# Low-part subtractions on GpSimd or VectorE, and the accumulators as halves of one tile, in a thresholded-attention and gated-mix kernel

## The chip, the cores and the metric

The kernel runs on one core of a Trainium2 chip. A core has five engines with queues of their own, each of which works through its instructions in order: TensorE (PE in the profile; PEld are its weight loads), VectorE (DVE), ScalarE (ACT), GpSimd (POOL) and SyncE (SP), which here only issues DMAs. Matrix products are summed in PSUM, everything else lies in SBUF. Engines wait for each other through semaphores: a counter that the one raises and the other waits for.

The metric is the device time of one execution in microseconds, as a median of several runs. The profile is of one execution.

## What is computed

```python
def _attn_ref(q, k, v, tau):                     # 8 batches, 8 heads, 576 x 64
    scale = 1.0 / np.sqrt(q.shape[-1])
    scores = scale * np.matmul(q, k.transpose(0, 1, 3, 2))
    thresh = np.max(scores, axis=-1, keepdims=True) - tau
    scores = np.where(scores >= thresh, scores, -1000000000.0)
    scores = scores - np.max(scores, axis=-1, keepdims=True)
    attn = np.exp(scores)
    attn = attn / (np.sum(attn, axis=-1, keepdims=True) + 1e-09)
    return np.matmul(attn, v)

def _moe_ref(x, w_val, conv_w, w_out):           # x: the heads side by side, 8 x 576 x 512
    ...
    for k in range(K):                           # K = 5, a causal convolution by channel
        gate_pre += conv_w[k][None, None, :] * xp[:, k:k + S, :]
    gate = 1.0 / (1.0 + np.exp(-gate_pre))
    val = x @ w_val
    return gate * val @ w_out
```

## The kernel before

Heads are worked in pairs: 8 batches of 4 pairs are 32 jobs. A job has 9 tiles of 128 query rows (four for each head, one for the 64 rows left over of both). For each tile PE multiplies queries by keys into a score tile `s` (L498), DVE takes the row maximum (L502), ACT the exponentials (L508) and the threshold (L510), DVE keeps the values over the threshold and sums them into `pp` or `pl` (L524), POOL or ACT divides (L554, L550), PE transposes by 128 columns into `tp` (L604) and ACT copies the result to `T` (L615). When half of a job's rows are there (320 or 256), PE multiplies `T` by `v` into an accumulator `acc` (L643, L650), and ACT evacuates it to `xT` (L658), the transposed output of the attention.

Then comes the mix, by batch. Each `xT` goes through the convolution's five taps (POOL L693, DVE L700) and the gate (ACT L708). PE makes two rounds of eight products of 12 matmuls each (L742): x by `w_val`, of which DVE makes g, gate times value (L769), and g by `w_out`, which ACT evacuates to `o` (L807). These too sum into `acc`, 320 or 256 columns at a time. So `acc` is written by 64 attention halves and 128 products, and is evacuated 192 times: 64 times by ACT L658, 64 by DVE L769, 64 by ACT L807.

Products are in float32 accuracy from parts of lower precision: a number is split into a high part (a rounded copy, made by ACT) and a low part (the number less its high part). `subtract` (L280 to L293) makes the low part, in two halves by column, of the keys (`kl`), the queries (`ql`), the attention's output (`xl`) and g (`gl`): 4 x 32 subtractions, 256 halves, all on POOL (L287).

No order is written out by hand. `op` notes an operation with the engines that may run it, a cost on each, a due time, what it comes after, and which buffers ("rooms") it takes and gives back. `carry_out` then plays it through with these costs: of all that can begin, it takes what can begin first, and among those the one with the earliest due time; the instructions are issued in that order. Where an operation has several ways (`other`), it goes to the engine on which it can begin first. POOL and the operations marked DVEp share one `port`: in the plan, only one of them runs at a time.

`Rooms` are buffers of one kind. `r_acc` has two tiles of 128 x 512 in PSUM, `acc0` and `acc1`; `take` hands out the one that came free first, `give` takes it back. The semaphore waits are not written in the kernel: the layer below adds them when it records the instructions, by which tile each reads and writes.

Of the kernel before, what the change touches and what calls it, by code (L numbers as in the profile page):

```python
# [10 lines left out]
F32 = mybir.dt.float32  # L11
# [4 lines left out]
ALU = mybir.AluOpType  # L16
# [5 lines left out]
DIVIDE = ("ACT",)  # L22
DUE = (8, 8, 8)
PACE_M = 0.17
# [3 lines left out]
def tile_thresholded_attention_gated_mix(  # L28
# [213 lines left out]
    class Words:  # L242


        def __init__(self, u, name, w, c, d0, before):
            due = u * 3.0 - 4
# [33 lines left out]
    def subtract(due, n, get, after, takes=(), gives=()):  # L280


        w = n // 2
        for cols in (slice(0, w), slice(w, n)):
            def run(cols=cols):
                dst, whole, high = get()
                nc.gpsimd.tensor_sub(dst[:, cols], whole[:, cols], high[:, cols].bitcast(F32))  # L287

            cost = w * 0.00237 + 0.04
            after = [op("POOL", due, cost, cost + 0.1, run, after, takes)]  # L290
            takes = ()
        after[0].gives = list(gives)
        return after[0]  # L293


    class Job:


        def __init__(self, i, b, g, at):
            self.i, self.b, self.g, self.at = i, b, g, at  # L300
            due = at - 9

            def fetch_v():
                self.v = r_v.take()
                nc.sync.dma_start(self.v, vs[b, g])

            self.got_v = op("SP", at - 3, 0.5, 3.6, fetch_v, takes=[r_v])
            if i == 0:
                self.load_at_once()
            else:  # L310
                self.prepare(due)

        def prepare(self, due):
# [28 lines left out]

            def scale_q():
                nc.gpsimd.tensor_scalar(self.q_r, self.q_r, sc, 0.0, op0=ALU.mult, op1=ALU.add)
# [5 lines left out]
            scaled = op("POOL", due, 0.75, 0.86, scale_q, [got_q])  # L350
            high = op("ACT", due + 1, 0.58, 0.76, high_q, [scaled], [r_qh])
            low = subtract(due + 2, S, low_q, [high], [r_ql], [(r_qr, lambda: self.q_r)])
# [94 lines left out]
    class Tile:  # L447
        def __init__(self, k, t, h, qc, grp):
# [21 lines left out]
            if TH == "ACT":  # L470
                after = [op("ACT", k - DUE[1], 0.83, 1.0, self.weigh, [largest], [r_e])]
            else:
                after = [
                    op("ACT", k - DUE[1], 0.64, 0.78, self.weigh, [largest], [r_e]),
                    op("DVE", k - 9, 0.13, 0.13, self.level, [largest]),
                ]
# [8 lines left out]
        def multiply(self):  # L485
            t, h, qc = self.t, self.h, self.qc
            s = self.s = r_s.take()
            for a in range(2):
# [17 lines left out]
        def weigh(self):  # L506
            self.e = r_e.take()
            nc.scalar.activation(self.e, self.s[:, :, :HS], AF.Exp, bias=self.nm[:, 0:1])  # L508
            if TH == "ACT":
                nc.scalar.activation(  # L510
                    self.nm[:, 1:2], self.nm[:, 0:1], AF.Identity, bias=less, scale=-1.0
                )

# [16 lines left out]
    class Group:  # L530
# [5 lines left out]
        def turned(self, k):  # L536
# [4 lines left out]
            add = op("POOL", k - 4, 0.2, 0.33, lambda: nc.gpsimd.tensor_scalar(  # L541
                sums(), sums(), 1.0, 1e-9, op0=ALU.mult, op1=ALU.add), [self.kept])
            inv = op("DVE", k - 4.9, 0.08, 0.33, lambda: nc.vector.reciprocal(ri(0, n), sums()), [add])  # L543
# [15 lines left out]
            for i in range(n):  # L559
                divided.append(op(  # L560
                    "POOL", k - 4 + 0.1 * i, 0.74, 0.82, divide(i, "POOL"), [inv],
# [3 lines left out]
            if self.both:  # L565
                divided.append(op("POOL", k - 4, 0.21, 0.3, lambda: spread(
# [3 lines left out]
            for c0, m in parts:  # L570
# [3 lines left out]
                    "PE", k - 3 + 0.1 * c0, 0.109 * m, 0.109 * (m - 1) + 0.35, self.turn(c0, m),  # L574
# [5 lines left out]
                if not half.begun:  # L580
                    takes, half.begun = [r_T], True
                out.append(op(
                    "ACT", k - 3 + 0.1 * c0, cost, cost + 0.17, self.copy(c0, m), [turn, *half.room], takes,
# [47 lines left out]
    class Half:  # L631
# [4 lines left out]
        def attended(self, k):  # L636
# [3 lines left out]
            def attend():  # L640
                acc = self.acc = r_acc.take()
# [17 lines left out]

            cost = 5 * w / 600 + 0.19  # L660
            gives = [(r_T, lambda: self.T)]
            if j == 1:
                gives.append((r_v, lambda: t.v))
            made = op("PE", k - 2, cost, cost + 0.2, attend, [t.got_v, *self.copies], [r_acc], gives)
            cost = 0.31 if j == 0 else 0.255
            after = [made] if j == 0 else [made, t.got_x]
            t.got_x = op("ACT", k - 4, cost, cost + 0.2, evacuate, after, [r_xT] if j == 0 else [],
                         [(r_acc, lambda: self.acc)])
# [185 lines left out]
    for t in jobs:  # L854
# [16 lines left out]
        convolve(t, batch, len(tiles))  # L871
        if t.g == NP - 1:
            last = products(batch, len(tiles) + 4.0, last)
# [44 lines left out]
```

## Time and profile before

| | |
|---|---|
| median of three runs | 766.35 us (765.61 to 766.81) |
| the profiled execution | 766.39 us |
| its span, first to last instruction | 764.6 us |
| busy: PE, DVE, ACT, POOL | 714.2, 617.5, 640.9, 544.1 us |
| mean granted clock of TensorE | 0.990 |

The page gives busy time, share of the span and the number of instructions for each engine; then the span in 40 slices of 19 us with the busy share of each in tenths; then groups of instructions by line, with busy time, mean length, and the idle time of the engine before them with what ended it. Records of PE's matmuls overlap, since the next begins before the last has left the array, so that "busy" tells that PE had work, not how fast it went.

### The profile page before, as it was taken

Reading aid. Unit: us, or ns where it says so; the run is one execution under the profiler, and the core shown is the slowest. Engines: PE = TensorE matmul, PEld = TensorE weight load, DVE = VectorE, ACT = ScalarE, POOL = GpSimd, SP = SyncE. Lnnn points to the kernel's source line nnn. Section 1 sums busy time; section 2 is a strip of 40 time slices with the busy share of each in tenths; the row PEclk is TensorE's granted clock in tenths of the full one; section 3 lists DMA queues with packets and bytes.
Section 4 is the critical chain, followed back from the end, with each engine's and each line's share of the span. In section 5 each row is a group of like instructions: output and inputs, shape, how many; then the busy total and the mean of one; then the engine's idle time right before and its main releaser. Section 6 shows DMA issues by size and latency. Waiting matters only on the chain.

```text
span 764.6 us, 15851 instructions
## 1 busy us (share of the span) xinstructions
PE 714.2 (93%) x5216; PEld 602.7 (79%) x5216; DVE 617.5 (81%) x1308; ACT 640.9 (84%) x1469; POOL 544.1 (71%) x885
## 2 busy tenths in 40 slices
PE   3687889979999999999999999999999999999997
PEld 3465557767788888888888888888888888888897
DVE  5878999989888878888888787888778988888630
ACT  5788987888889989989998898899889898988832
POOL 3677777778778867787678776688668876775431
PEclk9989999999999999999999999999999999999999
DMA  6746635344665556555555456455455455540001
GB/s 186 182 127 162 168 106 121 109 116 122 177 169 135 129 145 155 154 120 127 141 141 130 124 141 171 123 130 151 123 141 135 125 147 156 141 107 20 32 32 63
DMA packets 51890, 99.05 MB, mean 130 GB/s; under 512 B 9056, under 2 KB 9056, under 8 KB 51808
## 3 DMA queue, kind: packets, MB, share of 16 engines
q1 hardware_dynamic: 51488, 97.47, 49.0%
q8 instruction: 42, 0.69, 0.4%
q10 hardware_dynamic: 320, 0.56, 0.3%
q14 instruction: 40, 0.33, 0.1%
HBM read 35.74 MB, written 9.44 MB: 59 GB/s over the span
## 4 chain that ended last, share of the span: by engine, by line
PE 71%; DVE 8%; ACT 7%; POOL 6%; DMA 4%; issue 3%; SPq 1%; POOLq 0%; ACTq 0%
PE acc L742 20%; PE s L498 17%; PE acc L650 15%; PE tp L604 14%; PE acc L643 4%; DVE nm L502 3%; DMA q_r<-qT 2%; DVE pp L524 2%; ACT e L508 2%; ACT T L615 1%; DVE pre L700 1%; POOL pp L554 1%; POOL xl L287 1%; DMA KL<-kl 1%; POOL gl L287 1%
## 5 line engine op out<-in xcount | busy, mean ns | idle before, releaser
L502 DVE TENSOR_REDUCE nm<-s 128x1 f32<-128x576 f32 x288 | 215.8, 753 | 54.0 <-PE s L498 50.4
L508 ACT ACTIVATE e<-s,nm 128x576 f32<-128x576 f32 x288 | 215.5, 748 | 25.1 <-DVE nm L502 13.0
L524 DVE SCALAR_TENSOR_TENSOR pp<-s,nm,e 128x576 f32<-128x576 f32 x256 | 207.3, 813 | 35.1 <-ACT nm L510 31.7
L615 ACT COPY T<-tp 128x384 f32<-128x384 f32 x384 | 175.3, 487 | 27.6 <-PE tp L604 26.0
L604 PE MATMUL tp<-ident,pp 128*128 128x128 f32 x1152 | 182.3, 277 | 13.0 <-POOL pp L554 6.6
L498 PE MATMUL s<-KH,Q 128*128 128x288 f32 x512 | 162.1, 332 | 19.2 <-DVE Q L434 8.8
L554 POOL TENSOR_SCALAR pp<-pp,sums 128x576 f32<-128x576 f32 x174 | 142.5, 824 | 36.5 <-DVE sums L543 25.2
L604 PEld LDWEIGHTS tp<-ident,pp 128*128 128x128 f32 x1152 | 139.3, 142 | 23.2 <-POOL pp L554 10.1
L498 PE MATMUL s<-KL,Q 128*128 128x288 f32 x512 | 145.9, 299 | 0.7 <-DMA KL<-kl 0.7
L650 PE MATMUL acc<-T,v 128*64 128x256 f32 (+1 forms) x1024 | 138.3, 412 | 0.0
L498 PEld LDWEIGHTS s<-KH,Q 128*128 128x128 f32 x512 | 99.2, 194 | 43.3 <-DVE pp L524 13.8
L700 DVE SCALAR_TENSOR_TENSOR pre<-xT,cw,pre 128x576 f32<-128x576 f32 x128 | 119.2, 931 | 11.1 <-POOL pre L693 11.0
L650 PEld LDWEIGHTS acc<-T,v 128*64 128x64 f32 x1024 | 67.8, 136 | 62.9 <-issue 24.9
L498 PEld LDWEIGHTS s<-KL,Q 128*128 128x128 f32 x512 | 99.1, 194 | 0.9 <-DMA KL<-kl 0.9
L510 ACT ACTIVATE nm<-nm,less 128x1 f32<-128x1 f32 x288 | 85.0, 295 | 0.0
L742 PE MATMUL acc<-gl,woh 128*128 128x320 f32 (+1 forms) x256 | 78.1, 305 | 4.1 <-POOL gl L287 4.1
L742 PE MATMUL acc<-xl,wvh 128*128 128x320 f32 (+1 forms) x256 | 78.7, 307 | 2.6 <-POOL xl L287 2.5
L541 POOL TENSOR_SCALAR sums<-sums 128x2 f32<-128x2 f32 (+1 forms) x160 | 47.5, 297 | 45.5 <-DVE pp L524 33.2
L742 PE MATMUL acc<-gh,woh 128*128 128x320 f32 (+1 forms) x256 | 78.9, 308 | 0.7 <-ACT o L807 0.7
L742 PE MATMUL acc<-xh,wvl 128*128 128x320 f32 (+1 forms) x256 | 79.3, 310 | 0.0
L742 PE MATMUL acc<-xh,wvh 128*128 128x320 f32 (+1 forms) x256 | 78.4, 306 | 0.7 <-DVE g L769 0.5
L742 PE MATMUL acc<-gh,wol 128*128 128x320 f32 (+1 forms) x256 | 78.4, 306 | 0.0
(79 smaller groups left out, 1273.9 us busy)
## 6 DMA issues: line engine op xcount, KB each, us to landing
KH<-kh SPq DMA_DIRECT2D x124, 144.0 KB, 2.5
KL<-kl SPq DMA_DIRECT2D x124, 144.0 KB, 3.2
k_r<-kT SPq DMA_DIRECT2D x32, 320.0 KB, 3.7
v<-vs SPq DMA_DIRECT2D x32, 320.0 KB, 3.0
q_r<-qT SPq DMA_DIRECT2D x32, 288.0 KB, 2.9
outT<-o SPq DMA_DIRECT2D x32, 288.0 KB, 2.2
Q<-qh SPq DMA_DIRECT2D x62, 128.0 KB, 2.3
Q<-ql SPq DMA_DIRECT2D x62, 128.0 KB, 2.5
```

The lines of the kernel that those rows point to most:

```text
L498: nc.tensor.matmul(s[:, a, :HS], w, m, start=i == 0, stop=i == len(terms) - 1)
L502: nc.vector.tensor_reduce(self.nm[:, 0:1], self.s[:, :, :HS], axis=AX.XY, op=ALU.max, negate=True)
L508: nc.scalar.activation(self.e, self.s[:, :, :HS], AF.Exp, bias=self.nm[:, 0:1])
L510: nc.scalar.activation(self.nm[:, 1:2], self.nm[:, 0:1], AF.Identity, bias=less, scale=-1.0)
L524: nc.vector.scalar_tensor_tensor(grp.p[:, i * S : (i + 1) * S].rearrange("p (a f) -> p a f", a=2), self.s[:, :, :HS], self.nm[:, 1:2], self.e,
L541: add = op("POOL", k - 4, 0.2, 0.33, lambda: nc.gpsimd.tensor_scalar(sums(), sums(), 1.0, 1e-9, op0=ALU.mult, op1=ALU.add), [self.kept])
L554: nc.gpsimd.tensor_scalar(v, v, ri(i), 0.0, op0=ALU.mult, op1=ALU.add)
L604: nc.tensor.transpose(tp[:, i * P : (i + 1) * P], self.p[:, k0 : k0 + P], ident)
L615: nc.scalar.copy(T[:, c0 : c0 + n, self.off : self.off + P], tp[:, 0 : n * P].rearrange("p (c q) -> p c q", q=P),)
L650: nc.tensor.matmul(acc[hs, :w], t.v[:, c0 : c0 + D], T[:, h * NKC + c, :], start=False, stop=c == NKC - 1, skip_group_check=True,)
L700: nc.vector.scalar_tensor_tensor(cv, t.xT[:, i : i + S], cw[:, g, i : i + 1], cv, op0=ALU.mult, op1=ALU.add)
L742: nc.tensor.matmul(taken[name, e, j][:, :w], wt[:, c, c0 : c0 + P], moving(c, i)[:, hs], start=n == 0, stop=n == NM - 1,)
```

## The change

The two halves of each low-part subtraction get a second way, VectorE (as DVEp, with a cost of its own). The planner sends each half to the engine on which it can begin first. The diff carries more, of which most is switched so that it does what was done before: `EXTRA = 0`, `QS = False`, and constants (`AHEAD_D`, `LATE_M` and the like) with the values that stood in the code. One thing besides is not a switch: `r_acc` is now made of one tile of 128 x 2 x 512, and the two rooms that are handed out are its halves.

```diff
+SUB = True
+EXTRA = 0
+QS = False
...
-    r_s = Rooms(ps_s, 2, [P, 2, 512], F32, "s")
+    retired = []
+    r_s = Scores(ps_s, 2, [P, 2, 512], F32, "s")
     r_tp = Rooms(ps_t, 2, [P, 512], F32, "tp")
-    r_acc = Rooms(ps_a, 2, [P, 512], F32, "acc")
+    r_acc = Rooms(ps_a, 1, [P, 2, 512], F32, "acc")
+    if EXTRA:
+        r_s.extra = r_acc.take()
+        r_s.give(r_s.extra, 0.0)
+    else:
+        accs = r_acc.take()
+        for i in range(2):
+            r_acc.give(accs[:, i, :], 0.0)
...
         for cols in (slice(0, w), slice(w, n)):
-            def run(cols=cols):
+            def run(engine, cols=cols):
                 dst, whole, high = get()
-                nc.gpsimd.tensor_sub(dst[:, cols], whole[:, cols], high[:, cols].bitcast(F32))
+                engine.tensor_sub(dst[:, cols], whole[:, cols], high[:, cols].bitcast(F32))

             cost = w * 0.00237 + 0.04
-            after = [op("POOL", due, cost, cost + 0.1, run, after, takes)]
+            fast = w * 0.00116 + 0.07
+            after = [op(
+                "POOL", due, cost, cost + 0.1, lambda run=run: run(nc.gpsimd), after, takes,
+                other=[("DVEp", fast, fast + 0.12, lambda run=run: run(nc.vector))] if SUB else [],
+            )]
```

Lines move by the diff: L498 becomes L553, L604 L664, L658 L718, L742 L803, L769 L830, L807 L868, L287 L320. Of the 256 halves, 56 stand on VectorE in the new order (9 `kl`, 11 `ql`, 13 `xl`, 23 `gl`); four divisions move from POOL to ACT. With other costs in play the planner's whole order shifts: on every engine most rows stand elsewhere than before.

PE where the seventh batch's products by `w_val` reach their last block of columns (the first of its matmuls takes `xh0`; the row ahead of it is the last matmul of the product before). Names carry buffer numbers, and a bracket names the engine whose semaphore an instruction waits for. Before:

```order
L742 MATMUL acc1_106<-xh3_145,wvl_98 128x256
L742 MATMUL acc0_105<-xh0_142,wvh_97 128x320
L742 MATMUL acc0_105<-xl0_148,wvh_97 128x320
L604 MATMUL tp1_104<-ident_96,pl0_132 128x128 [waits Activation_49,Pool_49]
L742 MATMUL acc0_105<-xh0_142,wvl_98 128x320
L742 MATMUL acc0_105<-xh1_143,wvh_97 128x320
L742 MATMUL acc0_105<-xl1_149,wvh_97 128x320
L498 MATMUL s1_102<-KH0_117,Q0_115 128x288 [waits DVE_49]
```

The same place now:

```order
L803 MATMUL acc0_105<-xh3_144,wvl_98 128x256
L803 MATMUL acc0_105<-xh0_141,wvh_97 128x320
L803 MATMUL acc0_105<-xl0_147,wvh_97 128x320
L803 MATMUL acc0_105<-xh0_141,wvl_98 128x320
L803 MATMUL acc0_105<-xh1_142,wvh_97 128x320
L803 MATMUL acc0_105<-xl1_148,wvh_97 128x320 [waits DVE_49]
L553 MATMUL s1_102<-KH0_116,Q0_114 128x288
```

Both accumulators now have one name, `acc0_105`. The fifth matmul of the new product waits for DVE: by the semaphore's count, for the evacuation (L830) of the product before, which lies in the other half. That evacuation waits for PE to have done the fourth matmul of the new product, where before it waited for the twelfth of its own.

PE near the end of the program, where the products by `w_out` of the last batch follow each other without other work between them. Before, from one product's last three matmuls to the next one's first three:

```order
L742 MATMUL acc0_105<-gh3_161,woh_99 128x320
L742 MATMUL acc0_105<-gl3_165,woh_99 128x320
L742 MATMUL acc0_105<-gh3_161,wol_100 128x320
L742 MATMUL acc1_106<-gh0_158,woh_99 128x256 [waits Activation_49]
L742 MATMUL acc1_106<-gl0_162,woh_99 128x256
L742 MATMUL acc1_106<-gh0_158,wol_100 128x256
```

Now:

```order
L803 MATMUL acc0_105<-gh3_160,woh_99 128x320
L803 MATMUL acc0_105<-gl3_164,woh_99 128x320
L803 MATMUL acc0_105<-gh3_160,wol_100 128x320
L803 MATMUL acc0_105<-gh0_157,woh_99 128x256
L803 MATMUL acc0_105<-gl0_161,woh_99 128x256
L803 MATMUL acc0_105<-gh0_157,wol_100 128x256 [waits Activation_49]
```

The wait for ACT moved from the first matmul to the third, and it is for another evacuation: before, for the one of this same tile two products earlier; now for that of the product just finished.

The low parts of the last batch's g. Before, POOL's last rows of work:

```order
L693 TENSOR_SCALAR pre1_155<-xT1_141,cw0_172 128x576
L287 TENSOR_TENSOR xl1_149<-xT1_141,xh1_143 128x288 x2
L287 TENSOR_TENSOR gl0_162<-g0_156,gh0_158 128x288 x2
L287 TENSOR_TENSOR gl1_163<-g1_157,gh1_159 128x288 x2
L287 TENSOR_TENSOR gl2_164<-g0_156,gh2_160 128x288 x2
L287 TENSOR_TENSOR gl3_165<-g1_157,gh3_161 128x288 x2
```

Now DVE's last rows of work:

```order
L320 TENSOR_TENSOR gl0_161<-g0_155,gh0_157 128x288
L830 SCALAR_TENSOR_TENSOR g1_156<-pre1_154,acc0_105 128x320
L830 SCALAR_TENSOR_TENSOR g1_156<-pre1_154,acc0_105 128x256
L320 TENSOR_TENSOR gl1_162<-g1_156,gh1_158 128x288
L830 SCALAR_TENSOR_TENSOR g0_155<-pre1_154,acc0_105 128x320
L830 SCALAR_TENSOR_TENSOR g0_155<-pre1_154,acc0_105 128x256
L320 TENSOR_TENSOR gl2_163<-g0_155,gh2_159 128x288
L830 SCALAR_TENSOR_TENSOR g1_156<-pre1_154,acc0_105 128x320
L830 SCALAR_TENSOR_TENSOR g1_156<-pre1_154,acc0_105 128x256
L320 TENSOR_TENSOR gl3_164<-g1_156,gh3_160 128x288 x2
```

Five of these eight halves are DVE's now, one of each of the first three blocks and both of the last; POOL keeps three.

More of the change, by code (lines that the diff above doesn't have):

```diff
@@ L22 @@
 DIVIDE = ("ACT",)
+SUB = True
+EXTRA = 0
+QS = False
 DUE = (8, 8, 8)
+AHEAD_D = 4
+AHEAD_T = 3
+AHEAD_A = 2
+AHEAD_J = 9
+LATE_X = 0
+LATE_M = 4.0
+CONVERT = (3.0, -4)
 PACE_M = 0.17
@@ L176, in carry_out, with __init__, give @@
         assert not any(open_ops.values()), "some operations can never begin"
-    r_s = Rooms(ps_s, 2, [P, 2, 512], F32, "s")
-    r_tp = Rooms(ps_t, 2, [P, 512], F32, "tp")
-    r_acc = Rooms(ps_a, 2, [P, 512], F32, "acc")
+    class Scores(Rooms):
+        def __init__(self, *args):
+            super().__init__(*args)
+            self.extra = None
+        def give(self, room, when):
+            if self.extra is not None and room is self.extra and retired:
+                self.extra = None
+                for i in range(2):
+                    r_acc.give(room[:, i, :], when)
+            else:
+                super().give(room, when)
+    retired = []
+    r_s = Scores(ps_s, 2, [P, 2, 512], F32, "s")
+    r_tp = Rooms(ps_t, 2, [P, 512], F32, "tp")
+    r_acc = Rooms(ps_a, 1, [P, 2, 512], F32, "acc")
+    if EXTRA:
+        r_s.extra = r_acc.take()
+        r_s.give(r_s.extra, 0.0)
+    else:
+        accs = r_acc.take()
+        for i in range(2):
+            r_acc.give(accs[:, i, :], 0.0)
     r_kr = Rooms(raw, 1, [P, SK], F32, "k_r")
@@ L341, in low_q, with high_scaled, low_scaled @@
                 return self.ql, self.q_r, self.qh
+            def high_scaled():
+                self.qh = r_qh.take()
+                nc.scalar.mul(self.qh, self.q_r, sc)
+            def low_scaled():
+                self.ql = r_ql.take()
+                nc.vector.scalar_tensor_tensor(
+                    self.ql, self.q_r, sc, self.qh.bitcast(F32), op0=ALU.mult, op1=ALU.subtract
+                )
             def scale_q():
@@ L349, in prepare @@
             self.low_k = subtract(due + 1, SK, low_k, [self.high_k], [r_kl], [(r_kr, lambda: self.k_r)])
-            scaled = op("POOL", due, 0.75, 0.86, scale_q, [got_q])
-            high = op("ACT", due + 1, 0.58, 0.76, high_q, [scaled], [r_qh])
-            low = subtract(due + 2, S, low_q, [high], [r_ql], [(r_qr, lambda: self.q_r)])
+            if QS:
+                high = op("ACT", due + 1, 0.6, 0.78, high_scaled, [got_q], [r_qh])
+                low = op("DVEp", due + 2, 0.74, 0.87, low_scaled, [high], [r_ql], [(r_qr, lambda: self.q_r)])
+            else:
+                scaled = op("POOL", due, 0.75, 0.86, scale_q, [got_q])
+                high = op("ACT", due + 1, 0.58, 0.76, high_q, [scaled], [r_qh])
+                low = subtract(due + 2, S, low_q, [high], [r_ql], [(r_qr, lambda: self.q_r)])
             def place(which):
@@ L472, in __init__ @@
             else:
+                ways = {"ACT": (0.19, 0.33, self.level_act), "DVE": (0.13, 0.2, self.level)}
+                first, *rest = TH
                 after = [
                     op("ACT", k - DUE[1], 0.64, 0.78, self.weigh, [largest], [r_e]),
-                    op("DVE", k - 9, 0.13, 0.13, self.level, [largest]),
+                    op(first, k - 8.5, *ways[first], [largest], other=[(w, *ways[w]) for w in rest]),
                 ]
@@ L487, in multiply @@
             s = self.s = r_s.take()
+            if self.k >= EXTRA:
+                retired.append(self.k)
             for a in range(2):
@@ L540, in turned @@
             ri = lambda i, m=1: self.sums[:, 2 + i : 2 + i + m]
-            add = op("POOL", k - 4, 0.2, 0.33, lambda: nc.gpsimd.tensor_scalar(
+            add = op("POOL", k - AHEAD_D, 0.2, 0.33, lambda: nc.gpsimd.tensor_scalar(
                 sums(), sums(), 1.0, 1e-9, op0=ALU.mult, op1=ALU.add), [self.kept])
-            inv = op("DVE", k - 4.9, 0.08, 0.33, lambda: nc.vector.reciprocal(ri(0, n), sums()), [add])
+            inv = op("DVE", k - AHEAD_D - 0.9, 0.08, 0.33, lambda: nc.vector.reciprocal(ri(0, n), sums()), [add])
             divided = []
@@ L582, in turned @@
                 out.append(op(
-                    "ACT", k - 3 + 0.1 * c0, cost, cost + 0.17, self.copy(c0, m), [turn, *half.room], takes,
+                    "ACT", k - AHEAD_T + 0.1 * c0, cost, cost + 0.17, self.copy(c0, m), [turn, *half.room], takes,
                     [(r_tp, lambda c0=c0: self.tp[c0])],
@@ L640, in attend @@
             def attend():
-                acc = self.acc = r_acc.take()
+                acc = self.acc = rooms.take()
                 T = self.T[:, :, 0:w]
@@ L658, in evacuate @@
                 nc.scalar.copy(t.xT[:, x0 : x0 + w], self.acc[:, :w])
+            rooms = r_tp if EXTRA and t.b == 0 and k < EXTRA + 4 else r_acc
             cost = 5 * w / 600 + 0.19
@@ L663, in attended @@
                 gives.append((r_v, lambda: t.v))
-            made = op("PE", k - 2, cost, cost + 0.2, attend, [t.got_v, *self.copies], [r_acc], gives)
+            made = op("PE", k - AHEAD_A, cost, cost + 0.2, attend, [t.got_v, *self.copies], [rooms], gives)
             cost = 0.31 if j == 0 else 0.255
             after = [made] if j == 0 else [made, t.got_x]
-            t.got_x = op("ACT", k - 4, cost, cost + 0.2, evacuate, after, [r_xT] if j == 0 else [],
-                         [(r_acc, lambda: self.acc)])
+            t.got_x = op("ACT", k - AHEAD_A - 2, cost, cost + 0.2, evacuate, after, [r_xT] if j == 0 else [],
+                         [(rooms, lambda: self.acc)])
     class Batch:
@@ L870, in tile_thresholded_attention_gated_mix @@
             half.attended(len(tiles) - 1)
-        convolve(t, batch, len(tiles))
+        convolve(t, batch, len(tiles) + LATE_X)
         if t.g == NP - 1:
-            last = products(batch, len(tiles) + 4.0, last)
+            last = products(batch, len(tiles) + LATE_M, last)
     carry_out()
```

14 lines of the change are left out of this document (9 added, 5 removed).

## The prediction

> **What bounds the kernel now.** I read the page first: its busy times, then its slices of time.
>
> ```profile
> span 764.6 us, 15851 instructions
> ...
> PE 714.2 (93%) x5216; PEld 602.7 (79%) x5216; DVE 617.5 (81%) x1308; ACT 640.9 (84%) x1469; POOL 544.1 (71%) x885
> ...
> PE   3687889979999999999999999999999999999997
> ...
> DVE  5878999989888878888888787888778988888630
> ACT  5788987888889989989998898899889898988832
> POOL 3677777778778867787678776688668876775431
> ```
>
> TensorE (PE) is busiest, but the slices show stages. In the first nine or ten (19 us each) PE has gaps while VectorE (DVE) stands at 8 and 9; then PE is full until the last slice; in the last two or three the other engines have run out of work and PE alone goes on. A table of windows cut at these borders:
>
> ```profile
> core 0: us, PE busy (x) PEld busy (x) DVE busy (x) ACT busy (x) POOL busy (x), PEclk, DMA share, GB/s
> 0.00:180.00 180.00, 138.07 (x885) 106.89 (x887) 154.12 (x346) 145.34 (x332) 127.67 (x221) 0.96 0.55 143
> 180.00:716.00 536.00, 532.38 (x4010) 455.78 (x4007) 449.22 (x938) 477.37 (x1099) 402.21 (x649) 1.00 0.52 133
> ...
> 731.60:764.60 33.00, 28.25 (x211) 27.65 (x209) 7.70 (x12) 8.32 (x17) 9.06 (x11) 0.99 0.12 46
> ```
>
> In the middle stage PE idles 536.0 - 532.4 = 3.6 us, while GpSimd (POOL) has 134 us to spare and DVE 87. So there POOL's work is not what sets the time: taking some off it can win 3.6 us at most, and whatever makes PE wait there is paid in full. The waits of PE in that window say the same (who waits for whom: us in total, times, longest); they are all there is:
>
> ```profile
> PE s L498 <- DVE pp L524: 1.4, 4, 0.6
> PE tp L604 <- ACT T L615: 0.7, 2, 0.4
> PE acc L742 <- ACT o L807: 0.7, 1, 0.7
> PE acc L742 <- POOL gl L287: 0.6, 1, 0.6
> PE tp L604 <- POOL pp L554: 0.2, 1, 0.2
> ```
>
> The two waits on `acc` are 1.3 us together. Evacuating an accumulator costs PE nothing today, because the next group of matmuls goes into the other one.
>
> **The change, part 1: the subtractions.** Of 256 half subtractions, the order puts 56 on VectorE. The groups by line (busy us, mean ns of one, then idle time before):
>
> ```profile
> L287 POOL TENSOR_TENSOR xl<-xT,xh 128x288 fp32r<-128x288 f32 x64 | 59.1, 934 | 8.2 <-ACT xh L683 7.6
> L287 POOL TENSOR_TENSOR kl<-k_r,kh 128x320 fp32r<-128x320 f32 x64 | 55.7, 872 | 17.0 <-ACT kh L327 10.7 <-DMA KL<-kl 3.0 <-DMA Q<-ql 0.9
> L287 POOL TENSOR_TENSOR gl<-g,gh 128x288 fp32r<-128x288 f32 x64 | 54.4, 858 | 16.6 <-ACT gh L785 15.1
> L287 POOL TENSOR_TENSOR ql<-q_r,qh 128x288 fp32r<-128x288 f32 x64 | 52.5, 821 | 8.3 <-ACT qh L336 5.9 <-DVE sums L543 1.0
> ...
> L432 DVE TENSOR_TENSOR KL<-pp,KH 128x576 fp32r<-128x576 f32 x2 | 1.5, 758 | 2.2 <-ACT KH L426 2.2
> ```
>
> POOL loses about 56 x 0.87 = 49 us. VectorE has done one subtraction of this kind, 576 columns wide, in 0.758 us. Half the columns cost between half of that, 0.38, and the whole; I take 0.45, near the half, since the work is per column: 25 us more on DVE, 43 at most. Both fit into the 87 us that DVE has free in the middle, so neither shows.
>
> In the first stage, where POOL does hold PE up, the row is
>
> ```profile
> PEld tp L604 <- POOL pp L554: 9.6, 11, 2.0
> ```
>
> but only four of the 56 lie there (by their place among DVE's rows, against the 346 DVE records of that window). They can win 4 x 0.82 = 3.3 us of this, and cost DVE, the fullest engine there, 4 x 0.45 = 1.8 to 3.3. I take nothing, with 3.3 either way.
>
> At the end PE waits once for the last `gl`, the low part of g:
>
> ```profile
> 743.56 0.02 issue
> 743.58 0.43 DVE g L769
> 744.01 0.02 issue
> 744.04 0.68 ACT gh L785
> ...
> 749.51 0.04 issue
> 749.56 11.51 PE acc L742 x86
> ```
>
> That is the chain of waits (start, length, what); the timeline has PE's weight load at its end, with the idle time before it and what ended it in brackets:
>
> ```profile
> 749.55 0.19 PEld L742 LDWEIGHTS acc<-gl,woh 128*128 128x128 f32 x1 [1.43 <-POOL gl L287]
> ```
>
> With the halves of that chain split between two engines most of this 1.43 us goes: I take 1.2 us of gain.
>
> A row on the port that the two engines share: an instruction of DVE with two inputs in SBUF, the convolution's tap, is mostly even but at times far longer:
>
> ```profile
> L700 DVE SCALAR_TENSOR_TENSOR pre<-xT,cw,pre x128: 791/813/1461, 54.7 to 737.1; 128x576 f32<-128x576 f32 x128
> ```
>
> The Trainium skill (SBUF — State Buffer, section "SBUF: two separate sides") says that a VectorE instruction with two SBUF inputs and a GpSimd instruction that reads SBUF exclude each other for their whole length. The 1461 ns agree with it; by that rule the 3.3 us that part 1 could win in the first stage shrink to the difference of the two engines' times, about 1.5, which speaks against the change and leaves my zero as it is.
>
> **The change, part 2: the accumulators.** This is the part that decides. Before, `r_acc` held two tiles; now it holds the two halves of one tile. The planner hands them out as before, but the program's waits are attached per tile. In the new order (first two places above) the first matmul into the other half no longer waits for anything. Instead a matmul a few places further on waits for the evacuation of the half just finished, and that evacuation in turn waits not for its own last matmul but for the last one issued into either half before it. So matmuls and evacuation take turns where they used to overlap.
>
> The price of one such turn, with nothing else queued on PE in between, comes from these rows:
>
> ```profile
> 743.38 0.31 PE L742 MATMUL acc<-xh,wvh 128*128 128x320 f32 x1
> 743.53 0.31 PE L742 MATMUL acc<-xl,wvh 128*128 128x320 f32 x1
> ...
> 749.56 0.41 PE L742 MATMUL acc<-gl,woh 128*128 128x320 f32 x1 [1.21 <-POOL gl L287]
> 749.81 0.31 PE L742 MATMUL acc<-gh,wol 128*128 128x320 f32 x1
> ```
>
> From the start of the matmul that the evacuation waits for: 0.31 until it ends, 0.02 until the evacuation begins (743.56 to 743.58 above), 0.43 for the evacuation, 0.05 until PE starts (749.51 to 749.56), 0.25 until its next matmul: 1.06 us. Undisturbed, two matmuls take 2 x 0.145 = 0.29. So **a bare turn costs 0.77 us**; with 256 columns (0.28, and a step of 0.12) it is 0.79. I take 0.78. The evacuations by ACT are about as long:
>
> ```profile
> L807 ACT ACTIVATE o<-acc 128x320 f32<-128x320 f32 x64 | 26.7, 418 | 11.6 <-PE acc L742 11.3
> L658 ACT COPY xT<-acc 128x320 f32<-128x320 f32 x64 | 25.3, 395 | 22.7 <-PE acc L650 22.0
> ```
>
> How often? There are 192 evacuations (64 each of g, o and xT). For 185 of them the semaphore counts in the new order tell which matmul each waits for, and what PE does before the next matmul into `acc`. What lies between is scores and transposes, which go on meanwhile:
>
> ```profile
> 706.72 0.53 PE s L498 x4
> 707.25 0.12 PE acc L742
> 707.37 0.33 PE tp L604 x3
> ```
>
> - Middle: 137 evacuations. 53 have nothing in between (53 x 0.78 = 41.3). 17 have one group of transposes or scores or two groups of transposes, 0.33 to 0.66 us (4 x 0.45 + 8 x 0.25 + 5 x 0.13 = 4.5). The other 67 have 0.79 us or more and pay nothing. Sum 45.8 us.
> - End, where PE runs nothing but products: 21, of which 20 are bare and one has 0.33: 16.1 us.
> - First stage: 4 bare and 3 partly covered, 3.7 us by the same price; PE has 42 us of gaps there, so I take 1.0.
>
> What is queued behind a waiting evacuation? On DVE the row maxima and the thresholding of the next tiles, on ACT their exponentials; PE waits for these, but while PE itself stands still they are not late. No DMA is behind it, since SyncE issues them; the output's DMA merely leaves later.
>
> The Trainium skill (Perfetto Trace Analysis, section "Matmuls") says that independent groups of matmuls should rotate through different PSUM banks, so that the evacuation of one overlaps the matmuls of the next. The trace of before shows the rule at work (1.3 us of waits on `acc`), and the halves of the new tile lie 512 columns of 4 bytes apart, so by the rule alone the overlap would stay; that is rival B below.
>
> **Sum.** Span 764.6 + 45.8 + 16.1 + 1.0 - 1.2 (last gl) - 1.8 (half of the 3.6 us that PE idled in the middle takes up some turns) = 824.5. The profiled execution took 766.39 us, 1.8 more than its span and the same as the median of 766.35; with 1.8 the forecast is **826 us**.
>
> **Bounds of the price of a turn.** If PE restarted without the slow first step (0.25 back to 0.145) and the evacuation were the shortest seen, it is about 0.60: 33 + 12 = 45 us, and with all gains taken (3.3 + 3.6 + 1.6) 803 us. It is dearer where the evacuating engine is busy when the matmul ends:
>
> ```profile
> L769 DVE SCALAR_TENSOR_TENSOR g<-pre,acc x64: 394/441/490, 117.7 to 746.8; 128x320 f32<-128x320 f32 x32, 128x256 f32<-128x256 f32 x32
> ...
>   PE acc L742: 8.5, 12
> ```
>
> DVE was idle ahead of 12 of 64 of them; ahead of the other 52 it was at work on something else, whose groups take 0.75 to 0.93 us each on the page. Half of one on top makes 1.2: the same count then gives 79 + 25 = 104 us, about 870 us. I stay near the low row since an engine that PE keeps waiting catches up with its queue.
>
> **Rivals.**
> - **B, the halves stay independent in effect, and the change is faster.** The waits exist, but each is over before PE arrives, and POOL's relief counts. It needs evacuations within two matmul steps, 0.29 us, from which point on the turn is free; the shortest in the row above is 0.394. Time: 766.4 - 1.2 - 3.3 - 1.5 = about 760. Chance 0.03.
> - **C, turns at 1.2 us**, because evacuations stand behind other work in their in-order queue: 850 to 880, around 870. For it, the 52 of 64; against it, the end, where the queues are empty. Chance 0.14.
> - **D, part of the turns is absorbed**, because the planner's new order has PE late at those places anyhow: half of the middle's 45.8 us, so about 803, the case reaching from 780 to 803. Against it, PE's 3.6 us of idle time in the middle: there is little to absorb them. Chance 0.10.
> - **E, the change does little of what it says** (56 of 256 halves move) and the tile's waits are few: 766. Chance 0.01.
> - **The forecast**, 803 to 850: chance 0.72.
>
> The range 798 to 868 leaves out B and E, half of C and the lower part of D: 0.03 + 0.01 + 0.07 + 0.05 = 0.16. What a measurement of this kernel can tell from no change is about 0.2%, 1.5 us: faster 0.03, the same 0.01, slower 0.96.
>
> **What would show it.** The waits of PE on `acc` for DVE's g and ACT's o and xT should grow from 0.7 us in the middle to tens; at the end, each evacuation should go with a gap of about 0.5 us in PE's records (0.02 + 0.43 + 0.05); PE's busy share in the middle should fall to about 92%; DVE should show 56 subtractions of 0.4 to 0.8 us. If there are no such gaps at the end, part 2 is wrong; if they are there but the middle is longer or shorter than 46 us, it is the price of a turn or its cover that I have wrong.

## The result

| | us |
|---|---|
| before, measured beside it | 766.58 (765.61 to 766.82) |
| after, median of 4 runs | 839.24 (836.16 to 840.59) |
| after / before | 1.0945, 95% interval 1.0912 to 1.0977 |
| forecast | 826, range 798 to 868 |

The change makes the kernel 9.5% slower. The span grew from 764.6 to 838.8 us, 74.2 us, where the forecast counted 59.9. The head of the page after:

```profile
span 838.8 us, 15873 instructions
...
PE 746.4 (89%) x5216; PEld 612.9 (73%) x5216; DVE 643.4 (77%) x1364; ACT 649.7 (77%) x1473; POOL 501.6 (60%) x825
...
PE   4788778989889899999999998999999999999876
```

POOL does 42 us less, DVE 26 us more, and neither shows: every engine's share of the span is lower. The windows at the same times as before:

```profile
0.00:180.00 180.00, 141.15 (x842) 108.74 (x843) 147.83 (x331) 140.24 (x318) 117.93 (x200) 0.91 0.53 137
180.00:716.00 536.00, 500.91 (x3642) 416.49 (x3640) 431.16 (x899) 440.54 (x1002) 340.73 (x562) 1.00 0.49 127
```

In the middle PE idles 35.1 us where it idled 3.6, and gets through 3642 matmul records in place of 4010. The table of waits over the whole program says on what (before, evacuations had two rows in it, 0.7 and 0.5 us, one wait each):

```profile
PE acc L803 <- DVE g L830: 25.4, 46, 1.1
PE acc L803 <- ACT o L868: 18.8, 36, 0.9
...
PE acc L803 <- ACT xT L718: 0.9, 3, 0.5
```

That is 85 waits for 192 evacuations, and 45 us of idle PE. What one of them is, the timeline shows near the end, where PE has only products left (start, length, what, and in brackets the idle time before it with what ended it):

```profile
823.05 0.31 PE L803 MATMUL acc<-gh,wol 128*128 128x320 f32 x1
...
823.19 0.28 PE L803 MATMUL acc<-gh,woh 128*128 128x256 f32 x1
...
823.31 0.27 PE L803 MATMUL acc<-gl,woh 128*128 128x256 f32 x1
823.67 0.44 ACT L868 ACTIVATE o<-acc 128x320 f32<-128x320 f32 x1 [2.10 <-PE acc L803]
824.16 0.19 PEld L803 LDWEIGHTS acc<-gh,wol 128*128 128x128 f32 x1 [0.78 <-ACT o L868]
824.16 0.39 PE L803 MATMUL acc<-gh,wol 128*128 128x256 f32 x1 [0.58 <-ACT o L868]
```

The product of 320 columns ends with the matmul of 823.05. Two matmuls of the next product go into the other half; then PE stops. The evacuation of the 320 columns begins only at 823.67, when the second of these has ended, and the third matmul only when the evacuation is over. Nothing on ACT's side was late: ACT had been idle for 2.10 us. The chain of waits in that stretch shows the same turn over and over:

```profile
819.42 1.75 PE acc L803 x12
821.16 0.02 issue
821.18 0.39 ACT o L868
821.58 0.04 issue
821.62 1.98 PE acc L803 x12
823.60 0.03 ACTq L868
823.63 0.04 issue
823.67 0.45 ACT o L868
824.12 0.04 issue
824.16 1.75 PE acc L803 x12
```

Two products take 824.16 - 819.42 = 4.74 us, 2.37 each. Before, 86 matmuls in a row took 11.51 us, so 12 took 1.606. A bare turn (one with nothing else for PE to do) costs 0.76 us; the forecast had 0.78. The idle time in the list above is only 0.58 us of it: without a wait the next matmul begins before the record of the last one has ended. So the 45 us of the table understate what the turns cost.

### The profile page after: what moved, and what is told of

It is laid out like the page before. It is cut to its first block, busy times and chain, and to the rows that moved or that the text cites. A ratio compares the mean times of both kernels' runs of the same rounds, so it can differ in the third digit from the quotient of the medians.

```text
span 838.8 us, 15873 instructions
## 1 busy us (share of the span) xinstructions
PE 746.4 (89%) x5216; PEld 612.9 (73%) x5216; DVE 643.4 (77%) x1364; ACT 649.7 (77%) x1473; POOL 501.6 (60%) x825
## 4 chain that ended last, share of the span: by engine, by line
PE 71%; DVE 12%; ACT 9%; DMA 3%; issue 3%; POOL 2%; SPq 0%; DVEq 0%; ACTq 0%; POOLq 0%
PE acc L803 24%; PE s L553 16%; PE acc L710 14%; PE tp L664 13%; PE acc L703 4%; DVE g L830 3%; DVE nm L557 3%; DVE pp L584 3%; ACT e L563 2%; ACT o L868 2%; DMA q_r<-qT 1%; DVE pre L761 1%; ACT T L675 1%; DVE spare L262 1%; ACT nm L565 1%
## 5 line engine op out<-in xcount | busy, mean ns | idle before, releaser
L664 PE MATMUL tp<-ident,pp 128*128 128x128 f32 x1152 | 184.1, 280 | 8.2 <-POOL pp L614 3.5
L553 PE MATMUL s<-KH,Q 128*128 128x288 f32 x512 | 163.8, 334 | 26.9 <-DVE pp L584 14.5
L664 PEld LDWEIGHTS tp<-ident,pp 128*128 128x128 f32 x1152 | 141.5, 144 | 15.5 <-POOL pp L614 7.4
L553 PE MATMUL s<-KL,Q 128*128 128x288 f32 x512 | 148.2, 303 | 2.4 <-DMA KL<-kl 2.4
L553 PEld LDWEIGHTS s<-KH,Q 128*128 128x128 f32 x512 | 100.8, 197 | 50.8 <-DVE pp L584 20.7
L761 DVE SCALAR_TENSOR_TENSOR pre<-xT,cw,pre 128x576 f32<-128x576 f32 x128 | 114.8, 897 | 1.1 <-POOL pre L754 1.0
L710 PEld LDWEIGHTS acc<-T,v 128*64 128x64 f32 x1024 | 68.1, 137 | 63.8 <-issue 26.0
L553 PEld LDWEIGHTS s<-KL,Q 128*128 128x128 f32 x512 | 100.9, 197 | 2.6 <-DMA KL<-kl 2.6
L803 PE MATMUL acc<-xh,wvl 128*128 128x320 f32 (+1 forms) x256 | 80.6, 315 | 10.8 <-DVE g L830 9.8
L803 PE MATMUL acc<-xh,wvh 128*128 128x320 f32 (+1 forms) x256 | 81.1, 317 | 8.6 <-DVE g L830 8.4
L803 PE MATMUL acc<-gh,woh 128*128 128x320 f32 (+1 forms) x256 | 80.5, 314 | 8.8 <-ACT o L868 5.7
L803 PE MATMUL acc<-xl,wvh 128*128 128x320 f32 (+1 forms) x256 | 80.5, 314 | 5.9 <-DVE g L830 3.8
L803 PE MATMUL acc<-gl,woh 128*128 128x320 f32 (+1 forms) x256 | 80.1, 313 | 6.0 <-ACT o L868 4.7
L803 PE MATMUL acc<-gh,wol 128*128 128x320 f32 (+1 forms) x256 | 79.3, 310 | 6.6 <-ACT o L868 5.8
```

Source lines behind the costliest of these rows:

```text
L553: nc.tensor.matmul(s[:, a, :HS], w, m, start=i == 0, stop=i == len(terms) - 1)
L664: nc.tensor.transpose(tp[:, i * P : (i + 1) * P], self.p[:, k0 : k0 + P], ident)
L710: nc.tensor.matmul(acc[hs, :w], t.v[:, c0 : c0 + D], T[:, h * NKC + c, :], start=False, stop=c == NKC - 1, skip_group_check=True,)
L761: nc.vector.scalar_tensor_tensor(cv, t.xT[:, i : i + S], cw[:, g, i : i + 1], cv, op0=ALU.mult, op1=ALU.add)
L803: nc.tensor.matmul(taken[name, e, j][:, :w], wt[:, c, c0 : c0 + P], moving(c, i)[:, hs], start=n == 0, stop=n == NM - 1,)
```

## Where the time went, by place

Every kernel here makes the same 288 row maxima on DVE in the same order, so their starts in the traces are milestones. How much later than before (103.7, 176.2 and 719.3 us, span 764.6) each trace reaches the 37th, the 64th (at the border of the first stage) and the last:

| | 37th | 64th | last | span |
|---|---|---|---|---|
| after | +6.8 | +16.5 | +59.1 | +74.2 |
| two tiles, all else of after | +6.9 | +12.7 | +11.8 | +10.4 |
| halves of one tile, no subtraction on VectorE | -0.9 | +6.1 | +54.1 | +70.8 |

So after loses 16.5 us in the first stage, 42.6 in the middle (59.1 - 16.5) and 15.1 after the last row maximum. The forecast had 1.0, 44.0 and 14.9 (counting what it took off for PE's idle time and the last `gl`). The middle and the end are as forecast; the first stage is not.

The first two rows differ only in the accumulators, at nearly the same mean clock (0.981 and 0.980), so their difference is what the turns cost in this order: 3.8 us in the first stage, 43.5 in the middle, 16.5 at the end, 63.8 in all. The forecast's terms for turns were 1.0, 44.0 and 16.1. The experiments ask first whether the turns are the cause at all, then what happened in the first stage. The times of the kernel before, taken beside them, were 767.6 to 768.0 us.

## The experiments

### The two parts of the change, each alone

**Two tiles** (label e1_two_tiles): the change with `r_acc` as it was before. On every engine the instructions stand row for row as in the changed kernel.

```diff
-    r_acc = Rooms(ps_a, 1, [P, 2, 512], F32, "acc")
-    if EXTRA:
-        r_s.extra = r_acc.take()
-        r_s.give(r_s.extra, 0.0)
-    else:
-        accs = r_acc.take()
-        for i in range(2):
-            r_acc.give(accs[:, i, :], 0.0)
+    r_acc = Rooms(ps_a, 2, [P, 512], F32, "acc")
```

> The changed kernel with the two accumulators as two tiles again; every engine's order is the changed kernel's, row for row, only the waits on the accumulators are those of before. If the turns between matmuls and evacuations are the loss: 758 to 768 us, PE waits on acc under 5 us. If the new order or VectorE's 56 extra subtractions are the loss: 800 us or more, since both are still there. Something between, say 775 to 790, would give the order or the subtractions a share of their own, to be looked for in the first 200 us, where the changed kernel fell 10 to 17 us behind.

Measured: 774.97 us (769.13 to 776.81), ratio to before 1.0082 [1.0052, 1.0111]. The same order without the turns is 64 us faster. Of the 45 us its table of waits keeps only these two rows for evacuations (its lines are 7 lower than after's), and in its chain the last 86 matmuls run through again:

```profile
PE acc L796 <- ACT o L861: 1.0, 1, 1.0
...
PE acc L696 <- ACT o L861: 0.4, 1, 0.4
```

```profile
760.03 11.45 PE acc L796 x86
```

It was expected to take the time of the kernel before or less, though, and it is 7.4 us slower.

**Halves without the subtractions** (label e2_no_sub): the change with one switch off, so that the instructions stand row for row as in the kernel before.

```diff
-SUB = True
+SUB = False
```

> The changed kernel with all subtractions on GpSimd; every engine's order is that of the kernel before, row for row, only the accumulators are halves of one tile. If the turns are the loss: by the same count in this order (46 bare turns in the middle and 33 partly covered, 44.7 us; 16.1 at the end; 7.8 in the first stage by the full price) 766.6 + 60 to 72 = 827 to 839 us. If the order or the subtractions are the loss: 766 us.

Measured: 837.58 us (837.06 to 839.18), ratio 1.0909 [1.0871, 1.0946]. The form of the accumulators alone costs 70 us, in an order that is not changed at all. The Trainium skill (Perfetto Trace Analysis, section "Matmuls") asks for independent groups of matmuls to rotate through different PSUM banks, so that an evacuation overlaps the next group; here the groups go to and fro between two places 512 columns apart, and yet the overlap is gone. The two places must also be two to whatever sets the waits. The waits of this version:

```profile
PE acc L803 <- DVE g L830: 23.9, 45, 0.7
PE acc L803 <- ACT o L868: 16.8, 34, 0.6
```

Together the two runs rule out what one alone would leave open: that the planner's new order, or the work moved to DVE, makes PE wait. The parts do not quite add up: the new order costs 7 us with two tiles and 2 with halves, a difference near the spread of the runs (two tiles took 769.1 to 776.8).

### Is a turn made of the evacuation's length?

**Evacuations of `o` written twice**, once with halves (label e5_halves_o_twice: the version without subtractions) and once with two tiles (label e6_tiles_o_twice: the kernel before). The second copy writes the same values.

```diff
-                        nc.scalar.mul(o[f][:, hs], taken["wo", f, j][:, 0 : hs.stop - hs.start], 0.5)
+                        for _ in range(2):
+                            nc.scalar.mul(o[f][:, hs], taken["wo", f, j][:, 0 : hs.stop - hs.start], 0.5)
```

> The kernel of e2_no_sub (halves of one tile, all subtractions on GpSimd) with ScalarE's evacuation to o written twice, the second time the same over the first: 64 instructions more on ScalarE of about 0.42 us. If PE pays for each turn by the length of the evacuation, the same count with 1.2 in place of 0.78 for these 64 gives 15 us more in the middle, 4.6 at the end and up to 2 in the first stage: 855 to 861 us against the 837.6 of e2_no_sub. If what PE waits for is a fixed cost of the wait and not the evacuation: 836 to 842 us.

> The kernel before (two tiles) with the same doubling. With two tiles the next product runs on while the evacuation is under way, and ScalarE, 477 of 536 us busy in the middle, has room for 22 us more: 765 to 771 us. If ScalarE's added work were what costs: 785 us or more, and e5_halves_o_twice would have to be read less by as much.

Measured: 866.38 us with halves, 28.8 over the version without the doubling; 781.55 with two tiles (two runs), 13.8 over the kernel before (767.78 beside it). Both expectations were missed, on the high side. With two tiles nobody was expected to wait for the second copy, but the last row maximum comes 12.5 us later; the loss grows evenly through the middle, where ACT does 484.57 us of work in 536 in place of 477.37, and PE waits longer for ACT's other work (before, the wait in the second list was 0.7 us, in 2 waits):

```profile
180.00:716.00 536.00, 527.61 (x3911) 444.46 (x3908) 439.94 (x918) 484.57 (x1118) 395.53 (x638) 1.00 0.52 132
```

```profile
PE tp L604 <- ACT T L615: 3.5, 13, 0.4
```

So the pair is not clean in the middle: there the doubling costs by ACT's load as well. At the end ACT has nothing else to do. There two tiles lose 1.1 us to the doubling (13.6 - 12.5), and halves 7.0 (span of 863.1 against 835.4, less the 20.7 by which the last row maximum is later). The difference is 5.9 us; 13 evacuations of `o` begin after the last row maximum, each 0.41 us on average, 5.3 in all. The chain has both copies in it, one after the other, while PE stands:

```profile
851.22 0.45 ACT o L869
851.67 0.02 issue
851.69 0.45 ACT o L869
852.14 0.04 issue
852.18 1.74 PE acc L803 x12
853.92 0.02 issue
853.95 0.39 ACT o L869
854.34 0.02 issue
854.36 0.39 ACT o L869
854.75 0.04 issue
854.80 1.98 PE acc L803 x12
```

These rows are two products with their evacuations: they end at 854.80 + 1.98 = 856.78, 5.56 us after the first began, and the next evacuation follows 0.02 later, which makes 5.58. In the version without the doubling two products take 4.75 (816.10 to 820.85 in its chain). That is 0.42 more for each, the length of the second copy. So the length of the evacuation is part of the turn.

### Can the planner live with the turns?

**A planner that knows** (label e3_plan_knows): halves of one tile as in the change, but the planner lets no matmul into `acc` begin in its plan before a running evacuation has landed, and no evacuation before the last matmul into either half.

```diff
+                        held = [turn_[o.acc - 1]] if o.acc else []
-                        can.append((max([free, o.ready] + [r.free[0][0] for r in o.takes]), o))
+                        can.append((max([free, o.ready] + held + [r.free[0][0] for r in o.takes]), o))
...
+            if o.acc == 1:
+                turn_[1] = max(turn_[1], t + cost + 0.2)
+            elif o.acc == 2:
+                turn_[0] = max(turn_[0], o.landed)
```

> The changed kernel, still with the halves of one tile, but the planner is told of the turns: in its plan no matmul into an accumulator begins before the evacuation ahead of it has landed, and no evacuation before the last such matmul has ended. In the new order 9 bare turns are left, at the end, where nothing else is there to be done, and about 16 partly covered ones in the middle: 14 us by the price of 0.78. If the loss is bare turns, which other work of PE can cover: 778 to 795 us. If it is the waits as such, or lateness of the evacuating engines whatever stands between: 815 us or more.

Measured: 790.9 us (789.55 to 792.22), ratio 1.0297. It puts scores and transposes of other tiles where PE would stand, and the waits fall to

```profile
PE acc L812 <- DVE g L842: 5.6, 12, 1.0
...
PE acc L812 <- ACT o L880: 3.9, 7, 0.8
PE acc L710 <- ACT o L880: 2.4, 2, 1.6
```

Of the 23.1 us by which its span is longer than before's, 10.4 are lost up to the 64th row maximum, in the first stage. From there to the last row maximum it loses 1.1 us (10.4 to 11.5), and 11.6 at the end, where there is nothing to put between. That bears on the forecast's count: a turn is free where PE has other work for about 0.8 us, and the changed kernel paid so many because its plan took the halves for independent.

### What happened in the first stage?

Two tiles still lost 7 us. Three versions with two tiles divide the half subtractions by their due time (a row maximum's number): those below 72 are issued in about the first 200 us.

```diff
-                other=[("DVEp", fast, fast + 0.12, lambda run=run: run(nc.vector))] if SUB else [],
+                other=[("DVEp", fast, fast + 0.12, lambda run=run: run(nc.vector))] if due >= 72 else [],
```

is the late version (label e7_tiles_late, by its trace 42 halves on VectorE, where 40 were expected; the first 200 us are in the order of before); with `due < 72` it is the early one (e8_tiles_early, 7 halves); with `due >= 280` the last one (e9_tiles_last, 8 halves, where 7 were expected).

> Two tiles, and VectorE as a second way only for subtractions due at tile 72 or later, which is at about 200 us: 40 halves go there, and the order up to then is that of the kernel before, row for row. If e1_two_tiles lost its 8 us by the order of the first stage: 764 to 768 us. If it lost them by subtractions on VectorE wherever they are: 772 us or more.

> Two tiles, and VectorE as a second way only for subtractions due before tile 72: 7 halves go there, and the order up to about 200 us is that of the changed kernel, row for row. If the first stage's order is what e1_two_tiles lost by: 771 to 777 us, as much as e1_two_tiles, with a row maximum of tile 72 some 10 us later than in the kernel before. Otherwise 765 to 769 us.

Measured: late 766.12 us (763.36 to 768.32), ratio 0.9963 [0.9943, 0.9983]; early 780.34, ratio 1.0132 [1.0079, 1.0184]. So the loss comes in with the early halves, and seven of them cost more than all 56; more, too, than was expected of them. The early version reaches the 37th row maximum 6.1 us late, like after. By its trace only three of the seven begin ahead of the 64th row maximum: two of `kl` at 12.1 and 36.0 us, one of `gl` at 150.0.

The trace offered a cause. Before, POOL waits 3 us for the DMA that frees `kl`; in the early version VectorE does, with row maxima queued behind the wait:

```profile
POOL kl L287 <- DMA KL<-kl: 3.0, 1, 3.0
```

```profile
DVE kl L313 <- DMA KL<-kl: 3.1, 1, 3.1
```

To test it, three versions: early halves but none of `kl` (label e10_early_not_k, 4 halves), early halves of `kl` alone (e11_early_k, `n == SK`, 3 halves), and all halves but the early ones of `kl` (e12_not_early_k, `due >= 72 or n != SK`). The first of them:

```diff
-                other=[("DVEp", fast, fast + 0.12, lambda run=run: run(nc.vector))] if due < 72 else [],
+                other=[("DVEp", fast, fast + 0.12, lambda run=run: run(nc.vector))] if due < 72 and n != SK else [],
```

> Two tiles for acc; VectorE is offered only the halves with a due time below 72, and of these only ql, xl and gl: four go there (2 ql, 2 gl), none of kl. Theory K (what costs the first stage is a half of kl that waits in VectorE's queue for the DMA that frees kl, with row maxima behind it): 764 to 769 us, as the kernel before. Rival F (any half on VectorE, the fullest engine of that stage, costs it, or the other order lowers the granted clock whatever was moved): 771 to 780, with row maximum 72 over 5 us later than in the kernel before.

> The counterpart: VectorE is offered only the halves of kl with a due time below 72; three go there. Theory K: 773 to 781 us, with row maximum 36 some 6 us later than in the kernel before, as with all seven early halves. Rival F: three halves of seven, so about 3/7 of what the seven cost: 770 to 773.

> Two tiles; VectorE is offered every half but those of kl with a due time below 72. Theory K: 762 to 768 us, like the version in which it is offered only those due from 72 on (766.1). Rival F: 770 to 776, like the one with all halves (775.0).

| | median us | ratio | 37th | 64th | last | mean clock, median |
|---|---|---|---|---|---|---|
| all early (e8) | 780.34 | 1.0132 | +6.1 | +10.6 | +14.6 | 0.982 |
| early, not kl (e10) | 773.83 | 1.0076 [1.005, 1.0102] | +0.9 | +5.1 | +7.2 | 0.984 |
| early, only kl (e11) | 772.71 | 1.0053 [1.0026, 1.008] | +5.6 | +7.6 | +7.0 | 0.985 |
| all but early kl (e12) | 770.67 | 1.0043 [1.0027, 1.0059] | -0.6 | +3.6 | +5.8 | 0.986 |
| late (e7) | 766.12 | 0.9963 [0.9943, 0.9983] | -1.6 | -1.0 | -1.7 | 0.990 |

The theory of `kl` holds for the first 37 tiles: whoever has early `kl` halves on VectorE is 6 us late there, whoever has not is on time. As the cause of the whole loss it falls: without them 3 to 6 us are lost all the same, later, and at the last row maximum the version with only `kl` is no later than the one with early halves but none of `kl` (+7.0 and +7.2). Against the kernel before beside them, e10 lost 5.8 us, e11 4.7 and e8 12.6. These are not parts of one sum: with each switch the planner's order shifts, and by the traces e8 has four halves of `kl` and one each of `gl`, `ql` and `xl` on VectorE, e10 two of `ql` and two of `gl`, e11 three of `kl`. Rival F of the expectations fits the totals of e10, e11 and e12 (though it had the 73rd row maximum over 5 us late in e10, and it is 4.1), but it leaves open whether the work on VectorE, the order or the clock does it; which wait does it beyond the 37th tile was not found.

What the slower versions of this table and two tiles (0.984) share is a lower mean clock; the kernel before has a median of 0.991. TensorE's granted clock, taken from 200 to 716 us as one window, is 0.99 or 1.00 in each of these traces; it is lower ahead of that. By windows (the third column from the right), the kernel before, then two tiles, then early without `kl`:

```profile
40.00:80.00 40.00, 31.98 (x197) 23.75 (x196) 34.92 (x82) 35.20 (x83) 29.31 (x51) 0.91 0.55 145
80.00:120.00 40.00, 32.58 (x223) 23.64 (x222) 38.00 (x83) 34.44 (x82) 31.54 (x53) 1.00 0.59 151
```

```profile
40.00:80.00 40.00, 31.74 (x181) 23.45 (x181) 34.17 (x75) 32.32 (x75) 27.88 (x48) 0.84 0.57 149
80.00:120.00 40.00, 32.80 (x195) 23.32 (x196) 36.56 (x81) 32.70 (x74) 28.31 (x44) 0.88 0.48 121
```

```profile
40.00:80.00 40.00, 30.35 (x205) 21.78 (x205) 35.37 (x83) 35.41 (x83) 30.93 (x55) 1.00 0.71 171
80.00:120.00 40.00, 30.14 (x166) 21.14 (x164) 35.58 (x76) 30.14 (x70) 27.64 (x42) 0.82 0.47 130
```

With two tiles PE is busy for as long as before in these 80 us and has fewer matmuls done. The runs of one kernel let the clock's share be estimated, since their mean clock differs from run to run with the same instructions. At 0.993 the kernel before took 766.1 us (median of 13 runs) and two tiles 769.3 (of two); at 0.982 they took 772.0 (one run) and 775.6 (of two). By these two pairs, two tiles at one clock are 3 to 4 us slower than before, not 7; the rest goes with the clock, which is lower in most runs of that order. A straight line through all runs of each kernel gives 3.0 us between the two at 0.990. This is a correlation: no run here sets the clock, so that it is the cause is not shown. The Trainium skill (TensorE: Matmul & The Clock Gate, Part 1) says that the clock is held down when PE has not been busy of late. Between the stages the traces agree: the changed kernel's middle, with PE 93% busy, runs at 1.00, and the first 180 us, with 78%, at 0.91. Inside the first stage the windows above do not follow it: without early `kl`, PE has 30.35 us of work in 40 at a clock of 1.00 and 30.14 at 0.82. Nor does it take a long gap: in the two-tile trace PE's longest between 40 and 80 us is 2.1 us, at a clock of 0.84. What lowers it in one window and not in the next stays open.

### The queries scaled on other engines; the last subtractions alone

Two tiles with `QS = True`, another switch of the diff, by which ACT and DVE scale and split the queries without POOL (label e4_two_tiles_qs):

> The kernel of two tiles with one switch of the diff on (QS): the queries are scaled by ScalarE in the same step as the rounding, and their low part is made by one VectorE instruction, so that GpSimd loses its 32 scalings and the 64 halves of ql. A try at a version faster than both. PE is full in the middle stage, so only the first stage can gain: within 5 us of the kernel of two tiles; 5 us or more slower if VectorE, the fullest engine of the first stage, becomes the bound.

Measured: 773.04 us (768.84 to 776.56), ratio 1.007 [1.0043, 1.0097], 2 us from two tiles alone, as expected, and still 5.5 us slower than the kernel before. POOL's relief is worth nothing this way either. The last halves alone:

> Two tiles; VectorE is offered only halves with a due time of 280 or more: seven go there, and the order up to the last fifth of the run is that of the kernel before. If what the version with 40 late halves gained (1.4 us after the last row maximum) lies in the last subtractions, this one gains it too: 763 to 766.5 us against 766 to 767.5 for the kernel before. If it lies in the middle, this one takes the time of the kernel before.

Measured: 766.44 us, ratio 0.9987 [0.9971, 1.0003]. Its span is 0.4 us shorter than before's, and the late version's 3.1, of which 1.7 lie ahead of the last row maximum. What the late version gains is too little for these runs to say where it comes from. With 766.12 us against 767.78 for the kernel before beside it, the late version is the fastest here, and 73 us faster than the changed kernel.

## Why the forecast was right, and where it was off

- **What bounds the kernel**: right. PE is full in the middle, POOL's relief is worth next to nothing there (two tiles gain 0.9 us from the 64th to the last row maximum), and whatever makes PE wait is paid.
- **The price of a turn**: right, 0.76 us against 0.78. The doubled evacuations at the end, 0.42 us more for each product, show that the evacuation's length is one of the pieces that the forecast put together.
- **How many**: right for the middle and the end. The forecast counted 70 paying evacuations in the middle, 53 of them bare, and 21 at the end; the trace has 58 waits and 21, with the row maxima as borders. The turns cost 43.5 us there against 44.0, and 16.5 against 16.1.
- **A half on VectorE at 0.45 us, and 56 of them**: right, by the list of instructions of that line (least, median and most in ns; then first and last start):

```profile
L320 DVE TENSOR_TENSOR gl<-g,gh x23: 435/457/1126, 155.4 to 817.6; 128x288 fp32r<-128x288 f32 x23
L320 DVE TENSOR_TENSOR xl<-xT,xh x13: 445/455/1056, 205.5 to 795.4; 128x288 fp32r<-128x288 f32 x13
L320 DVE TENSOR_TENSOR ql<-q_r,qh x11: 440/452/787, 197.6 to 698.0; 128x288 fp32r<-128x288 f32 x11
L320 DVE TENSOR_TENSOR kl<-k_r,kh x9: 470/482/715, 12.3 to 622.3; 128x320 fp32r<-128x320 f32 x9
```

- **The last `gl`**: 1.05 us gained against 1.2; the weight load that idled 1.43 us now idles 0.38:

```profile
818.10 0.19 PEld L803 LDWEIGHTS acc<-gl,woh 128*128 128x128 f32 x1 [0.38 <-DVE gl L320]
```

- **The first stage**: mis-sized, by 15.5 us, and this is the whole error of 13 us. The forecast took 1.0 us for its turns and nothing, 3.3 either way, for its subtractions; it came to 16.5. The turns cost 3.8 us up to the 64th row maximum (after against two tiles), where 3.7 were counted at full price and cut to 1.0 since "PE has 42 us of gaps there": those gaps hid next to nothing. The new order alone costs 12.7 us there. The forecast priced the few early halves by their length, 0.4 to 0.8 us each; it had four of them there, and the trace has three (at 12.3, 36.7 and 155.4 us). What they changed was the order behind them, on the fullest engine of that stage, and the clock was lower with it. How the loss divides between order and clock beyond the estimate above stays open.
- **The rivals**: B (halves independent in effect, 760) fell with the runs on the two parts, as did E (766). For C (turns at 1.2 us) spoke the 52 of 64 evacuations of g that found DVE at work. It fell since DVE now sits idle for PE ahead of 50 of the 64, 29.6 us in all, as the second part of the list for the changed kernel's L830 says (engine and tile, us, times):

```profile
  PE acc L803: 29.6, 50
```

  That the engine for which PE waits catches up with its queue was the forecast's reason for the low price, and the 12 of before have become 50. D (half of the middle absorbed) did not come about; in these runs it took a planner that knows of the turns.

## What to carry to other kernels

Two accumulators are two only if the layer that sets the waits sees two: halves of one tile look the same in the memory and in a planner's books, and made matmul and evacuation take turns at 0.76 us each. Look at what each wait is attached to before counting on an overlap, and price a lost overlap as the whole turn, times the places at which the waiting engine has nothing else to do. Where an engine is full, work taken off another is worth little (here 0.9 us); and in a stage where several engines are nearly full, price a moved instruction by the order it upsets, not by its length.

## What was not expected

- A kernel's time goes with its mean granted clock, the instructions being the same: the kernel before ran in 764.95 us at 0.995, 766.1 at 0.993, 767.9 at 0.991 and 772.0 at 0.982. A version that ends 1% slower may owe half of it to the clock, if the clock is the cause; the two-tile estimate above is the only measure of that here.
- With two tiles, 51 more evacuations by ACT ahead of the last row maximum, most of them in a middle where ACT is 89% busy (477.37 of 536), cost 12.5 us there. Between 180 and 716 us PE idles 8.4 us in place of 3.6; where the rest lies was not found.
